# The first half of two weight matrices converted in pieces of 1024 columns, with the raw words in the empty second half

## The chip, the cores and the metric

The kernel runs on one core of a Trainium2 chip. The metric is the time of one execution in microseconds. TensorE (PE) multiplies matrices, VectorE (DVE) and ScalarE (ACT) work element by element, GpSimd (POOL) does small work and issues indirect transfers, and SyncE (SP) issues most transfers (DMAs). Each engine works its own list of instructions in order.

## The reference

Four batches, eight heads, 768 positions, head width 64. First comes linear attention with a decay per head (`lam`), which carries a 64x64 state from block to block:

```python
intra = einsum('bhic,bhjc->bhij', qb, kb) * Dmask
out[:, :, sl] = einsum('bhij,bhjd->bhid', intra, vb) + einsum('bhid,bhde->bhie', qb * lam_pow, kv_state)
kv_state = lam_block * kv_state + einsum('bhsd,bhse->bhde', kb * rev_pow, vb)
```

The heads are then laid side by side, so that x has the shape (4, 768, 512). The second part adds to x the real part of its two-dimensional Fourier transform, normalizes each row, and applies a two-layer network with a residual:

```python
u = x + real(fft(fft(x, axis=1), axis=2))
un = (u - mean(u)) / sqrt(var(u) + 1e-06)
out = u + maximum(un @ w_ch1, 0) @ w_ch2
```

`w_ch1` is 512x2048 and `w_ch2` 2048x512. Both arrive as 64-bit floating point numbers, while q, k, v and the result are 32-bit.

## The kernel before

**Attention.** A chunk is 128 positions of all eight heads; a batch has six. For a chunk, SP loads keys, queries and values (L263, two buffers each); PE transposes keys (L274) and queries (L279); ACT copies them out (kT L276, qT L281); DVE multiplies the queries by powers of the decay (qs L285). PE makes the scores (L298), DVE multiplies them by the decay (sc L302, two of 128x512 per chunk), PE adds the state's part (L315, L328) and the scores' part (L332) and ACT copies the output (oT L335), which PE transposes back (L348) for two ACT copies (L350, L351). Batch 0 builds mirrored rows in place; later batches write rows to DRAM (xa, xb) and gather them in reverse order with indirect transfers on POOL's queue (`mirror_a`, `mirror_b`).

**Mix and norm** (`fft_ln`). Symmetries fold the Fourier transform: DVE adds and subtracts mirrored rows (`fold_x` L418 to L422, and L462 to L472 in `fold_b`, in small steps), PE multiplies by tables of cosines and sines along the sequence (L508, copied by ACT, L512) and along the width (`width`, L521 to L526), and DVE adds the result to x (L588 to L592). `norm` takes statistics (L538, L539), POOL makes the reciprocal deviation (ve L542, rs L543), DVE writes the normalized row block `un` (L556), and PE transposes it (L561). `un` is one tile of 2 KB per partition in pool `np_`.

**The network.** The first four groups of 256 positions (PLAIN) are multiplied directly: w1 in L625, ReLU on DVE (L631) or ACT, w2 in L639. For the first three of them, w1's first 1024 columns and w2's first 1024 rows (`half[0]`) are worked through before the other half is needed. The other eight groups (LATE) use seven products in place of eight per block (L712, L759), in the second part of the run.

**The weights.** Both matrices stay in SBUF as 32-bit numbers, `w1` as 4 row blocks of 2048 columns and `w2` as 16 row blocks of 512. `weights()` hands out 32 pieces of 512 columns. For each, `load_weights` has SP load the raw words (`raw`, 512 KB, L209) into a buffer of pool `hp_`, which has four and serves the network's hidden tiles too; ACT takes the sign from the top 16 bits (L216); DVE masks the exponent (L217); ACT turns it into a power of two (L218); DVE joins power and sign (L220); and DVE makes the mantissa in three steps: the upper word (L222), the lower word added (L224), the scaling by the power (L225). Power and sign share one tile `e` of 2 KB per partition, out of a pool of two (`ep`), which also holds the transposed `un` (`uq`) of groups in LATE.

**The order.** Everything is written as generators that yield their cost in time units. `weave` runs a second generator beside a first in a given ratio, `beside` sets that ratio from two totals, and `part` stops after so many units. A piece of weights costs 1.0, of NW = 32 in all:

```python
run(beside(att0, NC * t_chunk - 2.7, w, 0.25 * NW))
run(beside(part(mix, T_FOLD), T_FOLD, att1, 2.5 * t_chunk))
run(beside(mix, 24.0, beside(att1, 3.5 * t_chunk, w, 0.12 * NW), 0.12 * NW + 2.5 * t_chunk))
run(beside(beside(chain(half[0]), t_half, w, 0.5 * NW), t_half + 0.5 * NW, fr, t_rest * t_half / t_back))
run(w)
```

So eight pieces lie beside the attention of batch 0, about four beside the mix of batch 0 and the attention of batch 1, sixteen beside the first halves of the network, and the rest follows. The framework then schedules the instructions of each engine from this program; a few (`keep_in_program_order`) keep their place in it.

Of the kernel before, what the change touches and what calls it, by code (L numbers as in the profile page):

```python
# [11 lines left out]
U32 = mybir.dt.uint32  # L12
U16 = mybir.dt.uint16
I16 = mybir.dt.int16
BF16 = mybir.dt.bfloat16
# [61 lines left out]
def kernel(  # L77
# [12 lines left out]
    DM = H * D  # L90
    DFF = moe_w_ch1.shape[1]
# [5 lines left out]
    KO = DM // 128  # L97
    FO = DFF // 128
# [16 lines left out]
    def front_pool(name, bufs):  # L115
        return front_end.enter_context(tc.tile_pool(name=name, bufs=bufs, side="left"))

    def plain_pool(name, bufs):
        return plain_end.enter_context(tc.tile_pool(name=name, bufs=bufs, side="right"))
# [4 lines left out]
    xn = front_pool("xn", HC)  # L124
    fp = front_pool("fp", 1)
    np_ = front_pool("np", 2)
    ep = front_pool("ep", 2)
    xp = plain_pool("xp", 2 * NC)
    up = plain_pool("up", 3)
    hp_ = plain_pool("hp", FO // 4)  # L130
# [6 lines left out]
    cnt = [0]  # L137

    def new(pool, shape, tag, **kw):
        cnt[0] += 1  # L140
        return pool.tile(shape, F32, tag=tag, name=f"{tag}{cnt[0]}", **kw)

    def psum_a(shape):
        return new(pa, shape, "pa")
# [41 lines left out]
    w1 = wt.tile([128, KO, DFF], F32, name="w1")  # L186
    w2 = wt.tile([128, FO, DM], F32, name="w2")

    w1v = moe_w_ch1.rearrange("(c p) f -> p c f", p=128)
    w2v = moe_w_ch2.rearrange("(c p) m -> p c m", p=128)  # L190
    WP = 512
# [5 lines left out]
        elif i == 2:  # L197
            nc.sync.dma_start(dt, cn["dt"].ap())

    def load_weights(dst, src):  # L200

        if src.dtype == F32:
            nc.sync.dma_start(dst, src)
            return
        raw = hp_.tile([128, 2 * WP], U32, tag="hr", name=f"raw{cnt[0]}")
        e = ep.tile([128, 2 * WP], U16, tag="e", name=f"e{cnt[0]}")
        pw, sg = e[:, 0:WP], e[:, WP:2 * WP].bitcast(BF16)
        cnt[0] += 1
        nc.sync.dma_start(raw, src.bitcast(U32))  # L209
        lo, hi = raw[:, 0:2 * WP:2], raw[:, 1:2 * WP:2]  # L210
        top = raw.bitcast(U16)[:, 3:4 * WP:4]
        d = dst.bitcast(U32)


        pin = tc.keep_in_program_order if late_words else lambda i: i
        pin(nc.scalar.activation(sg, top.bitcast(I16), AF.Sign))  # L216
        pin(nc.vector.tensor_scalar(pw, top, 0x7FF0, None, op0=ALU.bitwise_and))  # L217
        nc.scalar.activation(pw, pw, AF.Relu, bias=cvt[:, 0:1], scale=8.0)  # L218
        p = pw.bitcast(BF16)
        nc.vector.tensor_tensor(p, p, sg, op=ALU.mult)  # L220

        pin(nc.vector.tensor_scalar(d, hi, 0x000FFFFF, 0x00100000, op0=ALU.bitwise_and, op1=ALU.bitwise_or))  # L222
        del late_words[0:1]
        nc.vector.scalar_tensor_tensor(dst, lo, 2.0 ** -32, d, op0=ALU.mult, op1=ALU.add)  # L224
        nc.vector.scalar_tensor_tensor(dst, dst, 2.0 ** -20, p, op0=ALU.mult, op1=ALU.mult)  # L225
# [2 lines left out]

    def weights():

        for h in range(2):
            for f in range(h * DFF // 2, (h + 1) * DFF // 2, WP):
                for c in range(KO):
                    load_weights(w1[:, c, f:f + WP], w1v[:, c, f:f + WP])
                    yield 1.0
            for c in range(h * FO // 2, (h + 1) * FO // 2):
                load_weights(w2[:, c, :], w2v[:, c, :])
                yield 1.0


    xs, xn_, xd = {}, {}, {}
# [15 lines left out]
    first = const.tile([128, HP, 1], F32, name="first")  # L257
# [225 lines left out]
    def fft_ln(b):  # L483
# [19 lines left out]
        for i in range(5):  # L503
            ps = psum_a([128, 2, NK])
            m = 128 if i < 4 else 1
# [28 lines left out]
        def norm(g):  # L534
            mv = new(np_, [128, G, 2], "mv")
            for i in range(G):
                stt = new(np_, [128, 6], "stt")
                nc.vector.bn_stats(stt, xs[b, TT[g][i]])  # L538
                nc.vector.bn_aggr(mv[:, i, :], stt)  # L539
            ve = new(np_, [128, G], "ve")  # L540
            rs = new(np_, [128, G], "rs")
            nc.gpsimd.tensor_scalar(ve, mv[:, :, 1], EPS, None, op0=ALU.add)  # L542
            nc.gpsimd.tensor_tensor(rs, ve, mhalf, op=ALU.pow)  # L543

            yield 5.0 if (b, g) == PLAIN[0] else 1.0
            plain = (b, g) in PLAIN
            if plain:
                ut = uts[b, g] = new(up, [128, KO, G * 128], "ut")
            else:

                to = utd[b, g] = dram.tile([128, KO, G * 128], F32, name=f"utd{b}{g}")
            for i in range(G):
                un = new(np_, [128, DM], "un", bufs=1)
                u = xs[b, TT[g][i]]
                for o, x in ((un[:, 0:HM], u[:, 0:HM]), (un[:, HM:DM], u[:, DM - 1:HM - 1:-1])):
                    nc.vector.tensor_scalar(o, x, mv[:, i, 0:1], rs[:, i:i + 1],  # L556
                                            op0=ALU.subtract, op1=ALU.mult)
                if plain:
                    pt = psum_a([128, KO, 128])
                    for c in range(KO):  # L560
                        nc.tensor.transpose(pt[:, c, :], un[:, 128 * c:128 * c + 128], ident)  # L561
                    nc.scalar.copy(ut[:, :, 128 * i:128 * i + 128], pt)
                else:

                    uq = new(ep, [128, DM], "e")
                    nc.vector.transpose(uq, un)
                    for r in range(0, 128, 32):
                        dst = to[:, :, 128 * i + r:128 * i + r + 32].rearrange("(a d) c n -> d c a n", d=32)
                        src = uq[r:r + 32].rearrange("p (c a n) -> p c a n", c=KO, n=32)
                        nc.sync.dma_start(dst, src)  # L570
                yield 0.7
            if plain:
                return
            for T in TT[g]:
                ud[b, T] = dram.tile([128, DM], F32, name=f"ud{b}{T}")
                nc.sync.dma_start(ud[b, T], xs.pop((b, T)))

        for t in (1, 2, 0):
            ps = psum_a([128, DM])
            width(t, ps, False)  # L580

            A = halves(ps)[:, ::-1, 0:QM]
            B = bs[t % 2]
            nc.scalar.copy(B[:, 1:HM:2], ps[:, QM:HM])
            nc.scalar.copy(B[:, 2:HM:2], ps[:, HM + QM + 1:DM])
            ds = new(fp, [128, 2 * (HM + 2)], "ds")
            nc.scalar.copy(ds[:, HM:2 * HM + 2:HM + 1], ps[:, HM + QM:HM + QM + 1].broadcast_to([128, 2]))
            nc.vector.tensor_tensor(even_odd(ds[:, 0:HM]), A, even_odd(B[:, :]), op=ALU.subtract)  # L588
            nc.vector.tensor_tensor(even_odd(ds[:, HM + 1:2 * HM + 1]), A, even_odd(B[:, :]), op=ALU.add)
            u, v_ = xs[b, t], xs[b, HC + t]  # L590
            nc.vector.tensor_tensor(halves(u), halves(u), halves(ds)[:, :, 0:HM], op=ALU.add)
            nc.vector.tensor_tensor(halves(v_), halves(v_), halves(ds[:, 1:DM + 1])[:, ::-1, :], op=ALU.add)  # L592
            yield 1.6
            if t == 0:
                ps = psum_a([128, DM])
                width(HC, ps, True)
                x3 = xn_.pop((b, HC))
                nc.vector.tensor_tensor(even_odd(v_[0:1, 0:HM]), halves(ps[0:1])[:, ::-1, 0:QM],
                                        even_odd(x3[0:1, 0:HM]), op=ALU.add)
                nc.vector.tensor_tensor(v_[0:1, HM:DM:2], ps[0:1, 0:QM], x3[0:1, HM:DM:2], op=ALU.add)  # L600
                nc.vector.tensor_tensor(v_[0:1, HM + 1:DM:2], ps[0:1, HM + 1:HM + QM + 1],
                                        x3[0:1, HM + 1:DM:2], op=ALU.add)
                yield 0.9
            yield from norm(t)
# [218 lines left out]

    NW = 2 * KO * DFF // WP
    w = weights()
    t_chunk = 7.3
    t_front = NC * t_chunk + 13.0 + 7.0 + 5.7 + 3 * 2.4
# [67 lines left out]
```

## Time and profile before

| | |
|---|---|
| median of 6 runs | 831.14 us (828.64 to 833.05) |
| profiled execution | 832.98 us, span 830.9 us |
| PE busy | 800.1 us (96%) |
| DVE, ACT, POOL busy | 443.9, 182.7, 79.1 us |
| granted TensorE clock, mean | 0.995 |
| conversion of the weights on DVE (L217, L220, L222, L224, L225) | 14.4 + 15.2 + 13.8 + 23.2 + 23.0 us |
| conversion on ACT (L216, L218) | 21.9 + 23.0 us |
| raw pieces | 32 of 512 KB, 4.8 us from issue to landing (median) |

The span is the time from the first to the last instruction that the profiler saw; the time of an execution has some 2 us more. A row of a group gives line, engine, operation, tiles, shape and number, then busy time and mean duration in ns, then the idle time of the engine just before and what ended it. A row of stretches gives the time range, its length, and the busy time of each engine with its number of instructions. Matmuls overlap with the weight loads (PEld), so the two are not added.

### The profile page before, as it was taken

Reading aid. Unit: us, or ns where it says so; the run is one execution under the profiler, and the core shown is the slowest. Engines: PE = TensorE matmul, PEld = TensorE weight load, DVE = VectorE, ACT = ScalarE, POOL = GpSimd, SP = SyncE. Lnnn points to the kernel's source line nnn. Section 1 sums busy time; section 2 is a strip of 40 time slices with the busy share of each in tenths; the row PEclk is TensorE's granted clock in tenths of the full one; section 3 lists DMA queues with packets and bytes.
Section 4 is the critical chain, followed back from the end, with each engine's and each line's share of the span. In section 5 each row is a group of like instructions: output and inputs, shape, how many; then the busy total and the mean of one; then the engine's idle time right before and its main releaser. Section 6 shows DMA issues by size and latency. Waiting matters only on the chain.

```text
span 830.9 us, 11682 instructions
## 1 busy us (share of the span) xinstructions
PE 800.1 (96%) x4608; PEld 636.7 (77%) x4608; DVE 443.9 (53%) x1030; ACT 182.7 (22%) x436; POOL 79.1 (10%) x102
## 2 busy tenths in 40 slices
PE   7879889999999999999999999999999999999998
PEld 5767765757675867767748888888888888888886
DVE  6889879857853582245895551156312561145411
ACT  3654443125530210222101210022001210012100
POOL 3121140012010110220100000000000000000000
PEclk9999999999999999999999999999999999999999
DMA  9966542247861128430442011100111001110010
GB/s 264 247 136 183 143 131 77 85 116 188 224 169 39 51 55 161 107 124 19 114 109 94 1 51 51 51 1 0 52 51 51 0 1 38 33 32 1 1 39 25
DMA packets 126684, 68.87 MB, mean 83 GB/s; under 512 B 111151, under 2 KB 112175, under 8 KB 126631
## 3 DMA queue, kind: packets, MB, share of 16 engines
q1 hardware_dynamic: 121488, 55.67, 26.0%
q0 software_dynamic: 2112, 6.69, 2.4%
q10 hardware_dynamic: 3030, 5.78, 1.9%
q8 instruction: 36, 0.59, 0.3%
q14 instruction: 18, 0.14, 0.0%
HBM read 48.72 MB, written 19.40 MB: 82 GB/s over the span
## 4 chain that ended last, share of the span: by engine, by line
PE 80%; DVE 10%; issue 4%; DMA 3%; ACT 2%; POOL 1%; POOLq 0%; DVEq 0%; ACTq 0%
PE p L759 23%; PE p L712 23%; PE pm L639 10%; PE pm L625 7%; PE pa L332 3%; PE pa L508 3%; PE pa L298 3%; PE pa L328 2%; DMA x<-xb,ix 1%; PE pa L274 1%; PE pa L315 1%; PE pa L348 1%; DVE stt L538 1%; DMA xb<-xn 1%; PE pa L279 1%
## 5 line engine op out<-in xcount | busy, mean ns | idle before, releaser
L639 PE MATMUL pm<-w,hr 128*128 128x512 f32 x256 | 118.1, 605 | 1.3 <-DVE hr L631 1.3
L625 PE MATMUL pm<-ut,w 128*128 128x256 f32 x512 | 119.1, 382 | 0.2 <-DVE hr L631 0.2
L625 PEld LDWEIGHTS pm<-ut,w 128*128 128x128 f32 x512 | 94.3, 190 | 15.4 <-issue 3.1
L712 PE MATMUL p<-ur,w 128*128 128x256 f32 x384 | 93.8, 379 | 0.0
L639 PEld LDWEIGHTS pm<-w,hr 128*128 128x128 f32 x256 | 47.1, 192 | 51.5 <-issue 47.8
L712 PEld LDWEIGHTS p<-ur,w 128*128 128x128 f32 x384 | 73.0, 190 | 10.3 <-issue 0.5
L712 PE MATMUL p<-us,w1s 128*128 128x256 f32 x256 | 65.7, 379 | 0.0
L759 PE MATMUL p<-w,hs 128*128 128x256 f32 x256 | 58.0, 379 | 0.5 <-DVE y L780 0.5
L759 PE MATMUL p<-w,ha 128*128 128x256 f32 x256 | 57.9, 379 | 0.0
L759 PE MATMUL p<-w2s,hs 128*128 128x256 f32 x256 | 57.9, 379 | 0.0
L759 PEld LDWEIGHTS p<-w,hs 128*128 128x128 f32 x256 | 48.5, 190 | 7.5 <-DVE y L780 0.9
L759 PEld LDWEIGHTS p<-w,ha 128*128 128x128 f32 x256 | 48.6, 190 | 6.6
L759 PEld LDWEIGHTS p<-w2s,hs 128*128 128x128 f32 x256 | 48.6, 190 | 6.6
L712 PEld LDWEIGHTS p<-us,w1s 128*128 128x128 f32 x256 | 48.6, 190 | 6.6
L614 POOL DMA_INDIRECT out_dram<-y,ix x12 | 11.8, 987 | 408.3 <-DVE y L785 342.7
L739 ACT COPY ha<-p 128x256 f32<-128x256 f32 x32 | 11.9, 372 | 169.1 <-PE p L712 169.1
L332 PE MATMUL pa<-sc,v 128*64 128x128 f32 x384 | 32.8, 289 | 6.1 <-DVE sc L302 6.1
L750 DVE TENSOR_TENSOR ha<-p,ha 128x256 f32<-128x256 f32 x32 | 13.6, 425 | 44.8 <-ACT ha L749 44.8
L302 DVE TENSOR_TENSOR sc<-pa,decay 128x512 f32<-128x512 f32 x48 | 31.3, 683 | 11.5 <-PE pa L298 11.4
L298 PEld LDWEIGHTS pa<-qT,kT 64*128 64x128 f32 x384 | 26.1, 193 | 12.7 <-ACT qT L281 4.9
L332 PEld LDWEIGHTS pa<-sc,v 128*64 128x64 f32 x384 | 23.8, 141 | 15.0 <-DVE sc L302 10.0
L298 PE MATMUL pa<-qT,kT 64*128 64x128 f32 x384 | 30.8, 292 | 3.1 <-ACT qT L281 2.2
(144 smaller groups left out, 1134.9 us busy)
## 6 DMA issues: line engine op xcount, KB each, us to landing
raw<-in_moe_w_ch_dram SPq DMA_DIRECT2D x32, 512.0 KB, 4.8
k<-in_k_dram SPq DMA_DIRECT2D x24, 256.0 KB, 4.9
q<-in_q_dram SPq DMA_DIRECT2D x24, 256.0 KB, 4.9
v<-in_v_dram SPq DMA_DIRECT2D x24, 256.0 KB, 3.2
ud<-x SPq DMA_DIRECT2D x16, 256.0 KB, 2.3
utd<-e SPq DMA_DIRECT2D x64, 64.0 KB, 2.2
u<-ud SPq DMA_DIRECT2D x16, 256.0 KB, 2.6
ur<-utd SPq DMA_DIRECT2D x6, 512.0 KB, 4.1
```

The source lines that it names most:

```text
L298: mm(pss[hi][:, hp, :], lhsT=kT[HD[hi], hp, :], rhs=qT[HD[hi], hp, :], start=True, stop=True)
L302: nc.vector.tensor_tensor(t, pss[hi], decay[:, hi::2, :], op=ALU.mult)
L328: mm(po[HD[hi], hp, :], lhsT=s_old[HD[hi], hp, :], rhs=qs[HD[hi], hp, :], start=(hp == 0), stop=False, skip_group_check=True)
L332: mm(po[HD[hi], hp, :], lhsT=vt[:, 2 * hp + hi, :], rhs=sc[hi][:, hp, :], start=(c == 0 and hp == 0), stop=(hp == HP - 1), skip_group_chec ...
L508: mm = nc.tensor.matmul(ps[0:m, n, :], lhsT=piece(a, i, n), rhs=cs[0:rows, a, i in (2, 3), n, :], start=(a == 0), stop=(a == 1))
L614: nc.gpsimd.indirect_dma_start(out=out.rearrange("b s d -> (b s) d"), out_offset=row_of(2 + HC * (b + 1) + T - HC), in_=y[:, :], in_offset ...
L625: nc.tensor.matmul(ps, lhsT=w1[:, c, 128 * fc:128 * fc + 128], rhs=ut[:, c, :], start=(c == 0), stop=(c == KO - 1))
L639: nc.tensor.matmul(ps, lhsT=hr[(fc - f0) // 4][:, fc % 4, 128 * i:128 * i + 128], rhs=w2[:, fc, :], start=(fc == f0), stop=(fc == f1 - 1))
L712: nc.tensor.matmul(ps, lhsT=s2.A[a][:, kt, 128 * i:128 * i + 128], rhs=U[b][:, kt, :], start=(first and kt == 0), stop=(kt == 1), skip_gro ...
L739: nc.scalar.copy(a11, two(X))
L750: V.tensor_tensor(a22, two(Z), a22, op=ADD)
L759: nc.tensor.matmul(ps, lhsT=h[a][:, s, i, :], rhs=s2.B[b][:, i, :], start=(first and i == 0), stop=(i == HF - 1), skip_group_check=True)
```

## The change

The first half of the weights (w1's columns 0 to 1023 and w2's rows 0 to 1023) is converted in eight pieces of 1024 columns: one piece for each row block of w1 and one for two row blocks of w2. Such a piece yields 2.0 units. Its raw words, 1 MB, are loaded into places of `w1` and `w2` that belong to the second half and are filled only later; four such places are used in turn (`room`). The second half is converted in sixteen pieces of 512 columns as before, through `hp_`. Power and sign become tiles of their own, each of 2 KB per partition, and `un` moves from its own buffer in `np_` to the same pool `ep`, which now has three buffers for all of them. The SBUF in use is the same.

```diff
-    ep = front_pool("ep", 2)
+    ep = front_pool("ep", 3)
...
-    def load_weights(dst, src):
+    def load_weights(dst, src, raw):
 
         if src.dtype == F32:
             nc.sync.dma_start(dst, src)
             return
-        raw = hp_.tile([128, 2 * WP], U32, tag="hr", name=f"raw{cnt[0]}")
-        e = ep.tile([128, 2 * WP], U16, tag="e", name=f"e{cnt[0]}")
-        pw, sg = e[:, 0:WP], e[:, WP:2 * WP].bitcast(BF16)
+
+        def rows(t, n=WP):
+            return t if len(t.shape) == 3 else t.rearrange("p (r m) -> p r m", m=n)
+
+        dst, src, raw = rows(dst), rows(src), rows(raw, 2 * WP)
+        R = dst.shape[1]
+        pw, sg = (ep.tile([128, 2, WP], t, tag="e", name=f"{nm}{cnt[0]}")[:, 0:R]
+                  for nm, t in (("pw", U16), ("sg", BF16)))
         cnt[0] += 1
         nc.sync.dma_start(raw, src.bitcast(U32))
-        lo, hi = raw[:, 0:2 * WP:2], raw[:, 1:2 * WP:2]
-        top = raw.bitcast(U16)[:, 3:4 * WP:4]
+        lo, hi = raw[:, :, 0:2 * WP:2], raw[:, :, 1:2 * WP:2]
+        top = raw.bitcast(U16)[:, :, 3:4 * WP:4]
         d = dst.bitcast(U32)
...
-        for h in range(2):
-            for f in range(h * DFF // 2, (h + 1) * DFF // 2, WP):
-                for c in range(KO):
-                    load_weights(w1[:, c, f:f + WP], w1v[:, c, f:f + WP])
-                    yield 1.0
-            for c in range(h * FO // 2, (h + 1) * FO // 2):
-                load_weights(w2[:, c, :], w2v[:, c, :])
-                yield 1.0
+        F, K = DFF // 2, FO // 2
+
+        room = [w1[:, c:c + 2, F:DFF].bitcast(U32) for c in range(0, KO, 2)]
+        room += [w2[:, c:c + 4, :].rearrange("p c m -> p (c m)").bitcast(U32) for c in range(K, FO, 4)]
+        first = [(w1[:, c, 0:F], w1v[:, c, 0:F]) for c in range(KO)]
+        first += [(w2[:, c:c + 2, :], w2v[:, c:c + 2, :]) for c in range(0, K, 2)]
+        for i, (dst, src) in enumerate(first):
+            load_weights(dst, src, room[i % 4])
+            yield 2.0
+        second = [(w1[:, c, f:f + WP], w1v[:, c, f:f + WP]) for f in range(F, DFF, WP) for c in range(KO)]
+        second += [(w2[:, c, :], w2v[:, c, :]) for c in range(K, FO)]
+        for dst, src in second:
+            load_weights(dst, src, hp_.tile([128, 2 * WP], U32, tag="hr", name=f"raw{cnt[0]}"))
+            yield 1.0
...
-                un = new(np_, [128, DM], "un", bufs=1)
+                un = new(ep, [128, DM], "e")
```

Lines after `weights()` stand eleven lower in the changed kernel. In `load_weights` the sign is L221 there, the mask L222, the power L223, their product L225, the upper word L227, the lower word L229 and the scaling L230; the raw load is L214.

## The prediction, made before the changed kernel was run

> **What bounds the kernel now.** I read the page's totals first, then the busy time by stage, then the groups of the touched lines, the waits, and at last the chain that ended last inside the first stage. Totals:
>
> ```profile
> span 830.9 us, 11682 instructions
> PE 800.1 (96%) x4608; PEld 636.7 (77%) x4608; DVE 443.9 (53%) x1030; ACT 182.7 (22%) x436; POOL 79.1 (10%) x102
> ```
>
> TensorE is busy for 800.1 of 830.9 us, so no change to the conversion of the weights can win more than 30.8 us. Where that idle time lies is told by the busy time in six stretches (from:to, length, then busy PE, PEld, DVE, ACT, POOL, the granted TensorE clock, DMA share, GB/s):
>
> ```profile
> 0.00:20.00 20.00, 13.90 (x131) 10.80 (x132) 12.06 (x27) 6.93 (x13) 7.16 (x20) 1.00 1.04 258
> 20.00:60.00 40.00, 34.84 (x423) 28.21 (x421) 33.85 (x65) 26.10 (x61) 8.41 (x9) 1.00 0.82 190
> 60.00:100.00 40.00, 34.74 (x344) 28.33 (x339) 35.20 (x72) 18.64 (x43) 7.71 (x9) 0.96 0.61 159
> 100.00:160.00 60.00, 54.68 (x285) 39.29 (x284) 50.75 (x123) 18.86 (x43) 11.19 (x11) 0.97 0.33 106
> 160.00:240.00 80.00, 80.00 (x552) 55.00 (x551) 57.81 (x124) 32.10 (x63) 10.64 (x13) 1.00 0.66 172
> 240.00:831.00 591.00, 581.92 (x2889) 475.07 (x2887) 254.18 (x622) 80.02 (x214) 34.04 (x42) 1.00 0.18 50
> ```
>
> From 160 to 240 us TensorE has no idle time at all. The idle time that weights can touch is 6.1 us before 20 us, 5.2 us to 60, 5.3 us to 100 and 5.3 us to 160, together 21.9 us; in these stretches VectorE is busy for about 85% of the time, much of it with the conversion:
>
> ```profile
> L224 DVE SCALAR_TENSOR_TENSOR w<-raw,w 128x512 f32<-128x512 uint32 x32 | 23.2, 724 | 0.5
> L225 DVE SCALAR_TENSOR_TENSOR w<-w,e 128x512 f32<-128x512 f32 x32 | 23.0, 720 | 0.4
> L218 ACT ACTIVATE e<-e,cvt 128x512 uint16<-128x512 uint16 x32 | 23.0, 719 | 19.1 <-DVE e L217 18.6 <-ACT x L351 0.4
> L302 DVE TENSOR_TENSOR sc<-pa,decay 128x512 f32<-128x512 f32 x48 | 31.3, 683 | 11.5 <-PE pa L298 11.4
> L689 DVE TENSOR_TENSOR w<-w 128x1024 f32<-128x1024 f32 x4 | 4.7, 1220 | 0.0
> ```
>
> The reader should compare 683 ns for an operation of 512 columns with 1220 ns for one of 1024 (L689, a line the change doesn't touch). Last, three pieces of the chain that ended last, inside the attention of batch 0 (start, length, what):
>
> ```profile
> 16.66 0.61 DVE w L224
> ...
> 17.29 0.35 DVE w L225
> ...
> 17.90 1.29 DVE sc L302 x2
> 19.19 0.04 issue
> 19.23 1.10 PE pa L332 x14
> ...
> 28.55 0.62 ACT e L218
> ```
>
> Conversion instructions (L224, L225, L218) stand on this chain, ahead of the scores (L302) and of the key copy, because each engine works its list in order. They are not free here.
>
> **The change part by part.** Orders below are those of the compiled instruction lists of both kernels; times are from the one profiled execution of 832.98 us (span 830.9 plus 2.1 around it). Its median of six runs is 831.14, so I subtract from that what I find.
>
> *Fewer instructions.* Sixteen pieces of 512 columns become eight of 1024. Each pair had five VectorE and two ScalarE instructions twice and has them once: 40 and 16 fewer, and 8 fewer DMA issues on SP. Per VectorE instruction saved: by durations 2 x 0.685 (the shorter executions of L224) - 1.220 = 0.15 us; by the chain, where 512 columns take 0.60 us from start to start and L689 may overlap in the same way by 0.085 us, 2 x 0.60 - 1.135 = 0.07 us. So 2.8 to 6.0 us of VectorE; I take 0.08, that is 3.2 us, half in each group of four pieces, since most of these instructions run back to back. The 16-bit ones (L217, L220) have no row at 1024 columns; bounds by the rows are no gain at all, or a gain of their whole overlap-free fixed part, which the 0.07 and 0.15 hold. ScalarE: a copy of 512 columns has 0.59 us and one of 256 has 0.39, so about 0.19 is fixed and 16 x 0.19 = 3.0 us go.
>
> The Trainium skill weighs against this. Its page "VectorE: DVE Perf Modes", section "The TRN2 errata — SBUF-src ops pay a fixed extra latency per instruction", advises to cut tiles to at least 512 elements so that the fixed cost is spread, and pieces of 512 columns keep that already; by its 58 cycles at 0.96 GHz, an estimate, 40 x 0.060 = 2.4 us would go instead of my 3.2. The rows above come to nearly that at their lower end.
>
> *Attention of batch 0 (to 57 us).* Four double pieces stand where eight single ones stood. In chunk 1 sign and power (0.684 + 0.719 us at 512; taken as 2 x these less 2 x 0.19, so 2.4 us) now both stand ahead of the copy of qT, where only one sign of 0.68 stood: +1.7 us, and with the longer words ahead of qs and sc the output matmuls L332 of chunk 1 end +2.9 us later. After that VectorE has less to do: I followed the lists chunk by chunk with the durations above and found the copy oT (starts before: 20.4, 27.9, 35.3, 41.7, 49.3) at +2.9, +0.2, -0.9, -0.8, -2.0. I take **-1.6 us** at the end of the stage; at worst the 2.9 stays, at best the stage gets all of its 5.2 us of idle time less half, -2.6.
>
> *Transfers.* The first raw piece is 1 MB instead of 0.5, ahead of the second chunk's keys on SP's queue. At 258 GB/s, 0.5 MB are 1.9 us more; those keys landed about 1.7 us before TensorE needed them. I count 0.2 us into the 2.9 above; the bound is 0.5. In all the same bytes go. The raw words lie in w1's and w2's second half instead of the hidden tiles' buffers: the pieces that later overwrite those places come after 130 us, when the first ones are long done, so this costs 0 and buys 0 to 0.8 us (the 0.7 us L216 waited for L225, where a buffer was returned).
>
> *Around the norm of batch 0 (70 to 112 us).* Power and sign now are two tiles of one three-buffer pool which un and the transposed un use too; before, un had its own. So at most one piece is open while un is. In the new list VectorE converts piece 5 whole and does only the words L222 and L224 of pieces 6 and 7 there; their powers come after un. TensorE waits for un about 4.3 us in chunk 4 of batch 1 where it waited 1.45. POOL does all three pairs ve/rs of the norm before the gathers of mirror_a (before, two): a delay of 0.7 us each, and the fold L418 standing in order before the scores of the last chunk. The end of batch 1's attention and with it the write of xb and the gather (3.0 and 6.0 us) come about 7.6 us later. But TensorE has other work moved ahead meanwhile: 12 L625 and 8 L561, and nine L639 instead of one ahead of the first L508 of batch 1's mix, 8 x 0.86 = 6.9 us in pairs. 7.6 - 6.9 = **+0.7 us**. Bounds: -1 (chunks run as before and the filler saves) to +7.6.
>
> *Mix and norm of batch 1 (112 to 155 us).* This filler is missing now: the waits of L508 and L561 grow, **+1.2 us** (there are 5.3 us idle in 100 to 160; the L508 rows wait 3.0 at most in one place). On the other side VectorE has 2.5 us of pieces left before the next norm where it had some 11, and the second group of four pieces has its saving: **-1.6 us**. Bounds of this pair: -3 and +4.
>
> *Half clock.* The granted clock fell in two stretches of 3.4 us, at 72 and 126 us; eight L508 took 2.64 us there instead of 1.51. The change may shift either onto other work or call up a third, which costs up to 1.7 us. The Trainium skill, "TensorE: Matmul & The Clock Gate", section "What's actually happening", puts such stretches down to idle windows of TensorE; by that rule the longer wait for un would bring one, +1.7 us. I take 0, because the trace doesn't tell which wait called up either stretch.
>
> Sum: -1.6 + 0.7 + 1.2 - 1.6 = **-1.3 us**: 829.8 us against the median, 831.7 for a profiled execution. After 160 us the lists coincide again and TensorE is full; nothing more is won or lost there.
>
> **The rivals.**
> 1. *The saving lands whole.* All 40 instructions at 0.15 us lie on the path and the delay of chunk 1 is gone in chunk 2: -6.0, the filler even, no extra wait: +0.7: about -5.3, 825.8 us. For it speaks VectorE's 85% in the stretches with idle TensorE; against it that only about half of the idle time in these stretches ends with VectorE.
> 2. *The last words of w2 come too late (slower).* The nine L639 moved ahead need the pieces of w2's first half. Pieces 7 and 8 are asked for only behind batch 1's last keys and queries, near 75 us, and land near 82 to 84 (a 0.5 MB piece took 4.8 us, two of 1 MB share the queues). Their powers wait for one of three buffers behind un. If piece 8 is converted later than the end of the attention of batch 1 (about 117 us in the new order), these L639 stand still on TensorE, and all behind them. The 6.9 us of filler then is no filler: +6.9 with half a delay made up, about +4.5 us and 1.7 for a third half-clock stretch: up to +6, with 835.6 us for the middle. It decides from the point where piece 8 is finished after 117 us. For it speaks the buffer shared by four users; against it that VectorE needs only some 4.1 us for a piece.
> 3. *Nothing moves.* The saved instructions lie in time in which VectorE waits for ScalarE or TensorE (L302 alone waits 11.4 us for L298): 0 +- 1, 831.1 us.
>
> **How the numbers follow.** I give the forecast 0.42, rival 1 0.20, rival 2 0.30 and rival 3 0.08. The forecast's own range is 827 to 832.3. About 0.3% (2.5 us) is what a measurement of this kernel can tell from no change, so faster means below 828.6: rival 1 and a third of the forecast's case (0.15), together 0.35. Slower is above 833.6: rival 2 and a little of the forecast's case, 0.32; the rest, 0.33, is same. The range leaves out a tenth on each side: half of rival 1 below 825.5, and rival 2 beyond 836.5.
>
> **What would show it.** Right: the touched VectorE lines at 1024 columns have 1.1 to 1.25 us; the copy oT of chunk 1 starts later than 20.4 us by 2 to 3 and that of chunk 5 earlier than 49.3; TensorE waits 3 us or more for un near 90 us; L508 of batch 1 starts later than 125.9 us by 5 or more with nine L639 in front of it; TensorE is full from 160 us. Wrong: idle time of TensorE before L639 released by L230's words (rival 2), or an oT of chunk 5 that isn't earlier, or conversions at 1024 columns whose price is over twice that at 512.

## The result, and the profile after

The changed kernel takes 836.54 us (median of 20 runs, 835.75 to 839.63), the kernel before 831.71 us over the runs of the same days (46 runs). The medians are 4.8 us apart. The ratio, which is not the quotient of the medians, is 1.0067 (95% interval 1.0055 to 1.0079), or 5.6 us. A time of 829.8 us was forecast, 1.3 us faster than before, and 836.5 was the end of the range. The page of a profiled execution (835.98 us) begins:

```profile
span 834.2 us, 11613 instructions
PE 799.4 (96%) x4608; PEld 638.2 (77%) x4608; DVE 440.8 (53%) x990; ACT 179.3 (21%) x420; POOL 78.3 (9%) x102
```

VectorE and ScalarE do what the change says: 40 and 16 instructions fewer, 3.1 and 3.4 us less busy time in the two profiles. TensorE has the same work, yet the span is 3.3 us longer. Busy time by stretch, columns as before:

```profile
0.00:20.00 20.00, 11.87 (x119) 9.13 (x120) 11.98 (x24) 6.77 (x11) 7.76 (x19) 1.00 1.02 253
20.00:60.00 40.00, 35.47 (x438) 29.26 (x438) 32.76 (x49) 24.64 (x55) 9.60 (x9) 1.00 0.86 201
60.00:100.00 40.00, 32.65 (x319) 26.87 (x320) 36.22 (x64) 16.32 (x34) 8.02 (x9) 0.91 0.65 190
100.00:160.00 60.00, 54.27 (x275) 38.53 (x274) 43.31 (x102) 18.21 (x42) 7.82 (x11) 0.94 0.24 73
160.00:240.00 80.00, 80.00 (x557) 55.69 (x556) 61.37 (x132) 31.41 (x61) 10.98 (x13) 1.00 0.65 172
```

TensorE is busy 2.0 us less before 20 us and 2.1 us less between 60 and 100 us; the granted clock falls to 0.91 and 0.94 where it was 0.96 and 0.97. A busy time at a lower clock also holds less work (the sixteen L326 of chunk 4 take 1.12 us after, their counterparts L315 0.69 us before), so these rows understate the loss. Better marks are the starts of the copy oT, counted from the first one of the same profile (before, after): last chunk of batch 0 35.2, 35.4; batch 1's chunk 3 (chunks count from 0) 70.2, 69.6; chunk 4 80.3, 84.4; chunk 5 95.4, 112.8; first of batch 2 161.3, 165.9; last of batch 3 350.4, 354.5. The loss first shows between chunks 3 and 4, where 0.6 us ahead become 4.1 us behind, and 4.2 us are left at the end; the 17.4 us of chunk 5 are mostly made up. On TensorE's list that place reads (start, length, instruction, in brackets the idle time before it and what ended it):

```profile
84.63 0.60 PE L359 MATMUL pa<-ident,oT 128*128 128x128 f32 x4
85.54 1.16 PE L309 MATMUL pa<-qT,kT 64*128 64x128 f32 x16 [0.31 <-ACT qT L292]
91.06 1.09 PE L572 MATMUL pa<-ident,e 128*128 128x128 f32 x4 [4.36 <-DVE e L567]
92.08 1.12 PE L326 MATMUL pa<-v,kd 128*64 128x64 f32 x16
93.14 1.12 PE L572 MATMUL pa<-ident,e 128*128 128x128 f32 x4
94.19 1.97 PE L339 MATMUL pa<-qs,st 64*64 64x128 f32 x16
96.09 1.35 PE L343 MATMUL pa<-sc,v 128*64 128x128 f32 x16
```

The same place in the kernel before:

```profile
89.42 0.69 PE L315 MATMUL pa<-v,kd 128*64 128x64 f32 x16
90.03 1.09 PE L328 MATMUL pa<-qs,st 64*64 64x128 f32 x16
92.58 0.43 PE L332 MATMUL pa<-sc,v 128*64 128x128 f32 x2 [1.45 <-DVE sc L302]
93.24 1.09 PE L332 MATMUL pa<-sc,v 128*64 128x128 f32 x14 [0.23 <-DVE sc L302]
94.26 0.74 PE L561 MATMUL pa<-ident,un 128*128 128x128 f32 x4
```

Before, chunk 4's state (L315, L328) and output (L332) stand ahead of the transposes of un (L561), and fill the time in which the norm is made. After, the transposes (L572) come first, and TensorE stands still for 4.36 us with chunk 4's work behind them. Its masked scores (sc) were there by 89.93 us, 1.1 us before un's transposes could start:

```profile
88.61 0.66 DVE L313 TENSOR_TENSOR sc<-pa,decay 128x512 f32<-128x512 f32 x1
...
89.27 0.66 DVE L313 TENSOR_TENSOR sc<-pa,decay 128x512 f32<-128x512 f32 x1
90.51 1.38 DVE L567 TENSOR_SCALAR e<-x,mv,rs 128x256 f32<-128x256 f32 x4 [0.58 <-POOL rs L554]
91.80 0.69 DVE L227 TENSOR_SCALAR w<-w 128x1024 uint32<-128x1024 uint32 x1
...
115.28 0.69 DVE L222 TENSOR_SCALAR pw<-w 128x1024 uint16<-128x1024 uint16 x1
119.62 0.69 DVE L429 TENSOR_TENSOR fe<-fo,xn 128x512 f32<-128x512 f32 x1 [3.65 <-DMA fo<-xa,ix]
```

The last line is a second stall: chunk 5's scores stand behind a fold (L429) that waits 3.65 us for a gather, and L343 waits 3.33 us in turn. The new pieces themselves cost (busy time, then mean ns of one):

```profile
L230 DVE SCALAR_TENSOR_TENSOR w<-w,pw 128x1024 f32<-128x1024 f32 x8 | 10.4, 1297 | 0.1
L225 DVE TENSOR_TENSOR pw<-pw,sg 128x1024 bf16<-128x1024 bf16 x8 | 6.5, 808 | 3.4 <-ACT pw L223 3.4
L229 DVE SCALAR_TENSOR_TENSOR w<-w,w 128x1024 f32<-128x1024 uint32 x4 | 5.6, 1404 | 0.1
```

At 512 columns of the same kernel these have 688, 454 and 743 ns, so a long instruction costs somewhat under two short ones. The scaling and the lower word (1297 and 1404 ns) lie above the 1.1 to 1.25 us that the prediction gave.

### The profile page after: what moved, and what is told of

It reads as the page before. It is cut to its first block, busy times and chain, and to the rows that moved or that the text cites. A ratio compares the mean times of both kernels' runs of the same rounds, so it can differ in the third digit from the quotient of the medians.

```text
span 834.2 us, 11613 instructions
## 1 busy us (share of the span) xinstructions
PE 799.4 (96%) x4608; PEld 638.2 (77%) x4608; DVE 440.8 (53%) x990; ACT 179.3 (21%) x420; POOL 78.3 (9%) x102
## 4 chain that ended last, share of the span: by engine, by line
PE 80%; DVE 10%; issue 4%; DMA 3%; ACT 2%; POOL 1%; POOLq 0%; DVEq 0%; ACTq 0%
PE p L770 23%; PE p L723 23%; PE pm L650 10%; PE pm L636 8%; PE pa L519 3%; PE pa L343 3%; PE pa L309 2%; PE pa L339 2%; DMA x<-xb,ix 1%; PE pa L285 1%; PE pa L326 1%; PE pa L359 1%; PE pa L290 1%; DMA xb<-xn 1%; DVE sc L313 1%
## 5 line engine op out<-in xcount | busy, mean ns | idle before, releaser
L650 PE MATMUL pm<-w,hr 128*128 128x512 f32 x256 | 115.9, 597 | 1.3 <-DVE hr L642 1.3
L636 PEld LDWEIGHTS pm<-ut,w 128*128 128x128 f32 x512 | 95.7, 192 | 16.4 <-issue 3.8
L650 PEld LDWEIGHTS pm<-w,hr 128*128 128x128 f32 x256 | 46.7, 190 | 50.9 <-issue 47.4
L625 POOL DMA_INDIRECT out_dram<-y,ix x12 | 11.8, 988 | 407.3 <-DVE y L796 342.9
L343 PE MATMUL pa<-sc,v 128*64 128x128 f32 x384 | 31.9, 289 | 7.5 <-DVE sc L313 7.5
L313 DVE TENSOR_TENSOR sc<-pa,decay 128x512 f32<-128x512 f32 x48 | 31.2, 681 | 12.9 <-PE pa L309 12.9
L343 PEld LDWEIGHTS pa<-sc,v 128*64 128x64 f32 x384 | 23.6, 142 | 15.6 <-DVE sc L313 10.8
```

What stands on the lines that cost most here:

```text
L313: nc.vector.tensor_tensor(t, pss[hi], decay[:, hi::2, :], op=ALU.mult)
L343: mm(po[HD[hi], hp, :], lhsT=vt[:, 2 * hp + hi, :], rhs=sc[hi][:, hp, :], start=(c == 0 and hp == 0), stop=(hp == HP - 1), skip_group_chec ...
L625: nc.gpsimd.indirect_dma_start(out=out.rearrange("b s d -> (b s) d"), out_offset=row_of(2 + HC * (b + 1) + T - HC), in_=y[:, :], in_offset ...
L636: nc.tensor.matmul(ps, lhsT=w1[:, c, 128 * fc:128 * fc + 128], rhs=ut[:, c, :], start=(c == 0), stop=(c == KO - 1))
L650: nc.tensor.matmul(ps, lhsT=hr[(fc - f0) // 4][:, fc % 4, 128 * i:128 * i + 128], rhs=w2[:, fc, :], start=(fc == f0), stop=(fc == f1 - 1))
```

## The experiments

The theories, as they stood ahead of the first runs: A, a double piece's step of 2.0 units moves the order in which the program is written down, so that batch 1's chunks come too late; B, the pool shared by un, power and sign holds work up; C, the long instructions stand ahead of scores and qs. D (the half clock), E (raw words that land early) and F (raw loads that collide with other transfers) came up on the way. Each ratio is to the kernel before, run on the same chip, and is not exactly the quotient of the medians. Differences in us are between medians, some of them from different chips, where the medians of the kernel before lie between 831.45 and 832.17 us; where it matters, the difference of the ratios stands beside them.

**Two steps of 1.0 for a double piece.**

```diff
             load_weights(dst, src, room[i % 4])
-            yield 2.0
+            yield 1.0
+            yield 1.0
```

> The changed kernel, only that a double piece counts as two steps of 1.0 unit and not one of 2.0. In its list the gathers of batch 1 stand before the third norm of batch 0 again, and the transposes of chunk 5's keys come at row 255 of TensorE's list (254 before, 271 in the changed kernel). Theory A, the step of two units puts chunk 5 of batch 1 too late: the loss goes and the saving of the long instructions is left, ratio to before 0.994 to 1.000 (826.5 to 831.5 us), oT of chunk 5 near 108 us, the granted clock at half in two stretches as before. Theory B, the shared buffers of un, power and sign hold work up: no change against the changed kernel, 1.005 to 1.008. Theory C, the long instructions hold up scores and qs: also 1.004 to 1.008.

Measured: 833.61 us, 1.0025 (1.0007 to 1.0042). 2.9 us of the loss go (0.42% by the ratios), with every piece, buffer and instruction as in the changed kernel; not all of it, as theory A had said, so the result lies between its range and that of the others. TensorE's list:

```profile
88.61 1.09 PE L340 MATMUL pa<-qs,st 64*64 64x128 f32 x16
...
92.56 1.97 PE L344 MATMUL pa<-sc,v 128*64 128x128 f32 x14 [2.50 <-DVE sc L314]
94.46 1.53 PE L573 MATMUL pa<-ident,e 128*128 128x128 f32 x6
```

Chunk 4's output is ahead of the transposes again; it waits 2.50 us, where it was 1.45 in the kernel before.

**Steps of 2.0 in the kernel before.**

```diff
-                load_weights(w1[:, c, f:f + WP], w1v[:, c, f:f + WP])
-                yield 1.0
...
+        for i, (dst, src) in enumerate(todo):
+            load_weights(dst, src)
+            if i >= NW // 2:
+                yield 1.0
+            elif i % 2:
+                yield 2.0
```

> The kernel before, only that the first sixteen pieces of 512 columns are handed out two at a time in one step of 2.0 units. Pieces, buffers and instructions are those of before. Theory A: slower by as much as the changed kernel or a little more, since the saving isn't there: 1.006 to 1.011 (836.5 to 841 us), oT of chunk 5 of batch 1 after 120 us and the gather's wait ahead of the scores. Theories B and C: as before, 0.998 to 1.003.

Measured: 848.51 us, 1.0212 (1.0191 to 1.0234). The step alone, with short pieces and all old buffers, costs more than the whole change. The first transposes of un are ahead of chunk 4's output here too:

```profile
91.63 1.16 PE L301 MATMUL pa<-qT,kT 64*128 64x128 f32 x16 [0.31 <-ACT qT L284]
96.50 0.69 PE L564 MATMUL pa<-ident,un 128*128 128x128 f32 x2 [3.71 <-DVE un L559]
97.12 0.48 PE L318 MATMUL pa<-v,kd 128*64 128x64 f32 x2
```

Not all of this loss arises there: counted from the first oT, the last chunk of batch 0 is already 4.6 us later than in the kernel before (39.8 against 35.2), chunk 4 of batch 1 10.5 us later.

**Short pieces in the empty places.** The changed kernel with sixteen pieces of 512 columns.

```diff
...
-            load_weights(dst, src, room[i % 4])
-            yield 2.0
+            r = room[i % 4]
+            load_weights(dst, src, r[:, 0, :] if len(r.shape) == 3 else r[:, 0:2 * WP])
+            yield 1.0
```

> The changed kernel with its first half in sixteen pieces of 512 columns, one unit each, the raw words in the empty places of the second half, un, power and sign in the pool of three. Theory A: as before, 0.997 to 1.003, less the 0 to 0.8 us of waits for the raw buffers. Theory B: slower, 1.004 to 1.008. Theory C: as before.

**The pool of three alone, in the kernel before.**

```diff
-    ep = front_pool("ep", 2)
+    ep = front_pool("ep", 3)
...
-        e = ep.tile([128, 2 * WP], U16, tag="e", name=f"e{cnt[0]}")
-        pw, sg = e[:, 0:WP], e[:, WP:2 * WP].bitcast(BF16)
+        pw, sg = (ep.tile([128, 2 * WP], t, tag="e", name=f"{nm}{cnt[0]}")[:, 0:WP]
+                  for nm, t in (("pw", U16), ("sg", BF16)))
...
-                un = new(np_, [128, DM], "un", bufs=1)
+                un = new(ep, [128, DM], "e")
```

> The kernel before with power and sign as tiles of their own and un in the same pool of three; pieces of 512 columns in their old raw buffers, one unit each. Theory A: as before, 0.997 to 1.003. Theory B: slower, 1.004 to 1.008. Theory C: as before.

Measured: the places 835.28 us, 1.0038 (1.0018 to 1.0059); the pool alone 827.84 us, 0.9958 (0.9946 to 0.9970). Theory B falls with the wrong sign: the pool is a gain of 4.2 us (0.42% by the ratio). Between these two kernels only the place of the raw words differs, and it costs 7.4 us (0.80%). Theory C falls too: long pieces (two steps of 1.0, 1.0025) aren't slower than short ones in the same places (1.0038). VectorE of the kernel with places, ahead of the statistics of the first norm:

```profile
87.61 0.42 DVE L227 TENSOR_SCALAR w<-w 128x512 uint32<-128x512 uint32 x1
88.06 0.69 DVE L229 SCALAR_TENSOR_TENSOR w<-w,w 128x512 f32<-128x512 uint32 x1
88.67 0.68 DVE L297 TENSOR_TENSOR qs<-pa,qpow 128x512 f32<-128x512 f32 x1
89.28 0.42 DVE L227 TENSOR_SCALAR w<-w 128x512 uint32<-128x512 uint32 x1
...
90.27 0.68 DVE L229 SCALAR_TENSOR_TENSOR w<-w,w 128x512 f32<-128x512 uint32 x1
```

The words of two more pieces stand there. In units of 512 columns, the upper words ahead of the first statistics on VectorE's list are 12 in the kernel before and with the pool of three, 14 with four places used throughout, for long and short pieces alike and in the changed kernel. Theory E says that this early conversion delays the norm and the scores and so makes the loss.

**Idle matmuls in the two waits.** Ten and seven matmuls of 128x512 in the two longest waits of the changed kernel, then five and three; they write banks that the following matmuls overwrite.

```diff
                     pt = psum_a([128, KO, 128])
+                    for _ in range(10 if (b, g, i) == (0, 1, 0) else 0):
+                        nc.tensor.matmul(pt.rearrange("p c n -> p (c n)"), lhsT=ident,
+                                         rhs=decay[:, 0:4, :].rearrange("p h c -> p (h c)"), start=True, stop=True)
...
         po = psum_a([128, HP, C])
+        for _ in range(7 if (b, c) == (1, NC - 1) else 0):
+            mm(po.rearrange("p h c -> p (h c)"), lhsT=ident, ...
```

> The changed kernel with extra work for TensorE in its two longest waits: ten matmuls of 128x512 into the bank that the first transposes of un (L572 of batch 0) overwrite, and seven into the bank of the output of batch 1's chunk 5 before L339; the result is not used. Theory D, most of the loss is the clock that falls to half after these waits: with the waits filled the granted clock rises from 0.992 to 0.996 or more and the time falls by 1.7 us for each stretch of 3.4 us that goes, 830 to 834 us, ratio to before 0.998 to 1.003, though TensorE does 7 us more work. Rival, the loss is the waits themselves and the later chunk 5: no change or slower, 836 to 839 us, 1.005 to 1.009.

> The changed kernel with five and three idle matmuls in the two waits, where ten and seven proved too long: one takes 0.86 us, so 4.3 and 2.6 us lie in waits of 4.4 and 3.3 us. Their result is not used. Theory D, the clock at half costs most of the loss: granted clock 0.996 or more and 829 to 834 us, 0.997 to 1.002. Rival, at those places TensorE isn't what the end waits for, and its half clock costs little: 835 to 839 us, 1.004 to 1.009, whatever the clock.

Measured: 844.29 us, 1.0154 (1.0114 to 1.0194) with ten and seven, which took 15.1 us (8.85 and 6.28) where the waits had 7.7; 836.45 us, 1.0052 (1.0033 to 1.0071) with five and three. In the second one the first wait is filled to the tenth:

```profile
85.72 1.16 PE L309 MATMUL pa<-qT,kT 64*128 64x128 f32 x16 [0.32 <-ACT qT L292]
86.82 4.56 PE L575 MATMUL pa<-decay,ident 128*128 128x512 f32 x10
91.21 0.70 PE L578 MATMUL pa<-ident,e 128*128 128x128 f32 x4
```

and the clock from 84 to 100 us is 1.00, where it is 0.79 in the changed kernel; the rows of the changed kernel (first) and of this one:

```profile
84.00:100.00 16.00, 11.32 (x101) 9.49 (x100) 12.32 (x24) 6.57 (x15) 2.79 (x3) 0.79 0.34 80
...
84.00:100.00 16.00, 15.69 (x123) 11.50 (x122) 14.65 (x28) 6.87 (x16) 2.52 (x3) 1.00 0.35 82
100.00:130.00 30.00, 26.70 (x155) 19.63 (x154) 21.07 (x48) 12.82 (x24) 5.91 (x8) 0.94 0.37 110
```

Over the runs the mean clock was 0.995 to 0.998, against 0.989 to 0.994 of the changed kernel, and the median is the same to 0.1 us. Theory D falls as the main cause: with these two waits filled, hardly anything is won. The intervals of 1.0052 and 1.0067 overlap, and a small share of the loss isn't excluded.

This is shown for these two waits alone. Between runs of one kernel, time and clock do go together: the kernel before took 830.5 us (mean of 23 runs) at a clock of 0.998, 832.4 (53 runs) at 0.996 and 835.0 (3 runs) at 0.991. Whether the clock makes that difference or the waits that go with it isn't shown.

**Places only beside the attention of batch 0,** with long pieces for w1 and short ones for w2 (the diff shows this run), and with short ones for both.

```diff
-        first += [(w2[:, c:c + 2, :], w2v[:, c:c + 2, :]) for c in range(0, K, 2)]
...
-        second = [(w1[:, c, f:f + WP], ...
+        second = [(w2[:, c, :], w2v[:, c, :]) for c in range(K)]
+        second += [(w1[:, c, f:f + WP], ...
```

> The four pieces of w1 beside the attention of batch 0 have 1024 columns and lie in the empty places, in two steps of 1.0 unit each; w2's first half is in eight pieces of 512 columns in the old raw buffers, as before. Pool of three as in the changed kernel. Theory E, the empty places harm only beside the mix, where free places let the raw words of w2 land early and their conversion stand ahead of the norm: as fast as the pool of three alone, 0.994 to 0.998. If the places or the long instructions harm beside the attention too: 1.001 to 1.005 as with two steps throughout.

> Pieces of 512 columns throughout, one unit each, pool of three; the first eight (beside the attention of batch 0) have their raw words in the empty places, all others in the old raw buffers. Theory E: as the pool of three alone, 0.994 to 0.998. If the places harm wherever they are used: 1.002 to 1.006, as with all sixteen in them.

Measured: 830.05 us, 0.9986 (0.9961 to 1.0010), and 829.75 us, 0.9992 (0.9965 to 1.0020). Both lie between the two ranges that were expected. Against places throughout 3.6 and 5.5 us are won (0.39% and 0.46%), so the places harm beside the mix; whether they still cost something beside the attention these intervals don't tell. The wait of chunk 4's output falls back from 2.5 and 2.9 to 1.45 us, as theory E says, and long and short pieces don't differ beyond their intervals.

**Only un in the pool of three;** power and sign share a tile as before.

> The kernel before with un in the pool of now three buffers; power and sign still share one tile. If un's second buffer makes the gain of the pool of three (un's transposes no longer end the wait of the next un): 0.994 to 0.998 and the same clock of 0.999 to 1.000. If the separate tiles of power and sign make it: 0.998 to 1.003.

Measured: 828.92 us, 0.9983 (0.9958 to 1.0008). The interval reaches into both answers, and doesn't tell them apart.

**One place for w2's four pieces,** with two steps of 1.0 and with one of 2.0.

```diff
-            load_weights(dst, src, room[i % 4])
+            load_weights(dst, src, room[i % 4 if i < 4 else 0])
```

> All pieces of the first half have 1024 columns and count as two steps of 1.0 unit; w1's four use the four empty places in turn, w2's four all use the first one, so that the raw words of a piece can be loaded only when the one before it is converted. In VectorE's list 12 units of 512 columns then have their upper words (L227) ahead of the first statistics of batch 0's norm, as in the kernel before; with four places there were 14. Theory E, raw words that land early let conversion stand ahead of the norm: 0.995 to 1.000 (828 to 832 us), the wait of L332's counterpart in chunk 4 of batch 1 falls from 2.50 us to 1.5. Rival, the long instructions or the places as such cost the time: 1.001 to 1.005 as with four places, or more, since the transfers wait for one another.

> The changed kernel with its steps of 2.0 units, but w2's four pieces all in the first empty place: 12 units have their upper words ahead of the first statistics instead of 14, and batch 1's chunk 5 stays behind the third norm. If the step and the early words each cost their own part: 1.002 to 1.005, about half of the loss is left. If the late chunk 5 alone makes the loss: 1.005 to 1.009. If the early words alone make it: 0.996 to 1.001.

Measured: 830.75 us, 0.9987 (0.9970 to 1.0005), and 840.44 us, 1.0117 (1.0085 to 1.0149). The first number came true, its reason didn't: chunk 4's output waited 2.88 us, not 1.5. What fell was the wait of the first L520 of batch 1's mix, from 3.27 to 0.49 us. The second missed altogether; the two costs don't add. A likely reason stands in the profile of the second: SP issues a raw piece of 1 MB at 117.37 us, just after POOL's gather at 117.27 us. The transfers landing from 110 to 126 us say (size left out for gathers, then median time from issue to landing) of the changed kernel:

```profile
fo<-xa,ix POOLq DMA_INDIRECT x2, 3.3
```

and of the one with one place and steps of 2.0:

```profile
fo<-xa,ix POOLq DMA_INDIRECT x2, 6.1
```

VectorE waits 6.66 us at L429 there, and TensorE 6.60 us for the scores behind it.

**Batch 1 further ahead, steps of 2.0 kept.**

```diff
-    run(beside(mix, 24.0, beside(att1, 3.5 * t_chunk, w, 0.12 * NW), ...
+    run(beside(mix, 18.0, beside(att1, 3.5 * t_chunk, w, 0.12 * NW), ...
```

> The changed kernel with its steps of 2.0 units, but the mix of batch 0 counts 18 units where it counted 24 in the ratio of the two, so that batch 1's attention runs further ahead: chunk 5's keys are transposed at row 254 of TensorE's list (254 in the kernel before, 271 in the changed one), while the gathers of batch 1 still stand behind the third norm on GpSimd's list, and 14 units of upper words still stand ahead of the first statistics. If the late chunk 5 on TensorE is what the step of two units costs: 1.001 to 1.004, as with two steps of 1.0. If the late gathers, with the scores waiting behind L429, are what it costs: 1.005 to 1.008, as the changed kernel.

Measured: 832.28 us, 1.0011 (0.9994 to 1.0027). Other numbers of the order undo what the step does. The first range came true, its reason didn't: chunk 5's oT is at 111.8 us from the first, hardly earlier than the 112.8 of the changed kernel, since its scores still stand behind the waiting fold, and the last write of xb is as late as there (129.4 and 128.9 us). So a chunk 5 that late need not cost anything. Chunk 4 is at 77.9 instead of 84.4, and its output ahead of un:

```profile
91.71 1.09 PE L343 MATMUL pa<-sc,v 128*64 128x128 f32 x14 [1.24 <-DVE sc L313]
95.30 0.65 PE L572 MATMUL pa<-ident,e 128*128 128x128 f32 x2 [2.50 <-DVE e L567]
```

**Raw loads behind the write of xb.** Theory F: what the places and the pool also move are raw loads against the write of xb and its gather, on which batch 1's mix hangs. Two runs move only such loads, two of them in the long-piece kernel with two steps (the diff), and one in the kernel before, where the same is done for one piece of w2; the lists of all computing engines stay the same.

```diff
-        nc.sync.dma_start(raw, src.bitcast(U32))
+        queue.dma_start(raw, src.bitcast(U32))
...
-            load_weights(dst, src, hp_.tile(...))
+            load_weights(dst, src, hp_.tile(...), nc.scalar if i < 2 else nc.sync)
```

> The kernel with pieces of 1024 columns in two steps of 1.0, where the raw loads of the ninth and tenth piece (the first two of the second half, 512 KB each) are issued from ScalarE's queue behind the last write of xb of batch 1, and no longer from SP at 110 us just ahead of it. The lists of all computing engines are the same. Theory F, these transfers hold up the write of xb (5.94 us there, 1.24 with one place) and with it the gather and the first L520: the write falls to 1.2 to 2 us, the wait of 3.27 us at L520 goes, and the ratio to before is 0.996 to 1.000 (from 1.0025). Rival, the wait at L520 was hidden or comes back as a wait for the later pieces: 1.001 to 1.004.

> The kernel before, with one raw load moved: that of the fifteenth piece (512 KB), which SP issues at 110.0 us just ahead of the write of xb, comes from ScalarE's queue behind that write. The lists of all computing engines are the same. Theory F: write and gather of 3.0 and 6.0 us fall to about 1.3 and 3.5, the wait of 3.02 us at L508 goes, 0.995 to 0.998, as with the pool of three. Rival, the pool of three gains by something else and this wait is made up for later: 0.999 to 1.002.

Measured: 828.01 us, 0.9959 (0.9941 to 0.9977), from 1.0025; and 827.97 us, 0.9963 (0.9946 to 0.9980). Waits (total, times, longest) from 108 to 140 us, with the loads ahead of xb:

```profile
POOL x L456 <- DMA xb<-xn: 5.5, 1, 5.5
PE pa L520 <- DVE fe L479: 3.3, 1, 3.3
DVE fe L430 <- DMA x<-xb,ix: 2.7, 1, 2.7
```

behind it, in the long-piece kernel:

```profile
POOL x L457 <- DMA xb<-xn: 1.6, 1, 1.6
```

and in the kernel before with its one load moved, where L508 had waited 3.0 us for L467 and L418 2.9 us for the gather:

```profile
PE pa L508 <- DVE fe L467: 0.4, 1, 0.4
DVE fe L418 <- DMA x<-xb,ix: 0.3, 1, 0.3
```

There the load is now issued behind the write:

```profile
115.02 0.33 ACTq L362 DMA_DIRECT2D xb<-xn  x1
116.56 0.34 ACTq L209 DMA_DIRECT2D raw<-in_moe_w_ch_dram  x1
```

Theory F holds: one transfer of 512 KB at the wrong place cost the kernel before 3.5 us (0.37%; 0.20 to 0.54%). With the loads out of the way, the long-piece kernel and the kernel before come out alike (0.9959, 0.9963), though they differ in pieces, places and pool. These two kernels and the pool of three (0.9958) beat both the kernel before and the changed one.

For theory E little is left with long pieces: the run with the two loads moved still has 14 units of upper words ahead of the first statistics, chunk 4's output still waits 2.3 us, and it is as fast as the pool of three alone, which has 12. What the places cost a long-piece kernel is thus put down to the colliding loads. For short pieces this wasn't run.

## Why the prediction was wrong

*Fewer instructions* (3.2 us of VectorE): right as a price, 3.1 us less busy time measured. The Trainium skill's estimate from "VectorE: DVE Perf Modes" was 2.4, so both were near. None of it can be seen in the time: where long and short pieces can be compared with nearly all else equal (1.0025 and 1.0038, 0.9986 and 0.9992), they differ by no more than their intervals, which are nearly as wide as the saving. (The prediction gave VectorE's busy share in the four early stretches as 85%; by its rows it is 82%.)

*Attention of batch 0* (-1.6 us): wrong. Chunk 1 is 3.2 us later than before (2.9 forecast), but the stage ends 0.2 us later, not 1.6 earlier. My walk through the list gave the saving on VectorE to the path; counted from the first oT, chunks 3, 4 and 5 are 0.3, 1.0 and 0.2 us later, where 0.9, 0.8 and 2.0 us earlier were forecast.

*Around the norm* (7.6 - 6.9 = +0.7 us): this is the step that failed, by most of the error. Its parts were seen: TensorE's wait for un was forecast as 4.3 us and is 4.36; the nine L639 ahead of the first L508 are there. What failed is the cover: I set 6.9 us of L639, with 12 L625 and 8 L561 besides, against the delay, but these come after the wait, and chunk 4's own work stands behind it too, so that nothing fills it. Chunk 4 ends 4.1 us late. Chunk 5 is 17.4 us late where 7.6 was forecast, because the fold waiting for the gather stands ahead of its scores; I had named that order and priced it at 0.7 us per norm. From chunk 5 to batch 2, 12.9 us are regained, where my terms (-6.9, +1.2, -1.6) gave 7.3. Forecast and measured sums at batch 2: -1.3 and +4.5. Of the two late chunks, the run with batch 1 further ahead points at chunk 4: there chunk 5 is 16.4 us later than before, chunk 4 isn't late, and the kernel is as fast as before.

*The cause behind it* had no line in the forecast at all: the diff's step of 2.0 units. I compared the lists and took their differences as the effect of pieces and buffers, where the step alone lets the first norm overtake chunk 4 and costs 2.9 us here; in the kernel before it costs 16 us, though there part of it, 4.6 us in its profile, is lost ahead of batch 1.

*The pool of three* was booked as a burden and is worth 4.2 us by itself. A likely reason stands in its profile: the raw loads come at 115.3 us, behind the gather of xb at 113.9, and VectorE's wait for that gather is gone, which alone is worth 3.5 us in the kernel before. That this is the whole gain isn't shown. *Transfers* (0.2 us, "this costs 0" for the places): wrong beside the mix, by 3.6 to 5.5 us, with long pieces because of the colliding loads.

*Half clock* (0): the stretches did come, 0.79 from 84 to 100 us after a wait of 4.4 us, as the Trainium skill, "TensorE: Matmul & The Clock Gate", section "What's actually happening", leads one to expect. The length of the wait alone doesn't decide it here: with one load moved in the kernel before, the clock fell to half from 93 to 99 us after a wait of 1.45 us (0.53 from 92.8 to 99.8), and in the kernel before itself it stayed at 1.00 after the same wait. The price I feared for one, 1.7 us, hardly shows at the two filled waits; elsewhere it isn't measured.

*The rivals.* Rival 2 had the sign and nearly the size (835.6), for another reason: no L650 waited more than 0.2 us for w2's words. Rivals 1 and 3 are excluded.

The parts, as differences of the ratios along one chain of kernels (before, pool of three, short pieces in the places, long pieces in two steps, changed): pool of three -0.4%; empty places +0.8%, most of it beside the mix; long for short pieces -0.1%, within the error; step of 2.0 +0.4%. They add up to the measured +0.7% by construction; the order of the parts matters, as the run with one place and steps of 2.0 shows.

Open: which share of the pool's gain is un's second buffer (with it alone the raw loads come behind the gather of xb too, at 114.6 and 113.5 us, but the time doesn't tell); which of the two harms of the places, early words or colliding loads, weighs more with short pieces; and how much of what the pool and the moved loads win is the half clock that goes with the wait (from 100 to 130 us 0.94 in the kernel before, 1.00 with the pool or with the load moved). Moving chunk 4's work ahead of un, or chunk 5's scores ahead of the waiting fold, and nothing else, wasn't tried.

## What to carry to other kernels

When a change also alters how much a generator hands out at a time, look first at what it does to the written order: compare only the steps, with all work unchanged, before pricing the work. At a wait on the bound engine, look at what stands behind the waiting instruction and was ready; only work listed ahead of it is cover. And when a transfer chain (write, gather, fold) sets a stage, look at which bulk loads are issued within a few microseconds of it: moving one of them was worth as much as anything else here.

## What the runs showed of the hardware

The two gathers of rows of xa took 3.3 us to land (median) in the changed kernel, with the last raw load issued 6 us before them, and 6.1 us with a 1 MB load issued 0.1 us after the first. A 256 KB write of xb took 3.0 us in the kernel before, with a raw load of 512 KB issued 3.1 us ahead of it, and 5.9 us behind two such loads (the kernel with two steps of 1.0); with no raw load issued in the 10 us before it, 2.0 to 2.1 us (changed kernel, one place, load moved). The 1.24 us expected for one place are only a piece of a chain. Ten matmuls of 128x512 in 32 bits in a row took 8.85 us and show as twenty records. TensorE's granted clock from 84 to 100 us was 1.00 instead of 0.79 when its wait was filled with idle matmuls, and the median stayed the same to 0.1 us.
